# Planner thresholds per stage instead of per kernel, new rates and priorities, and a later padding memset in a two-layer attention-plus-mixer kernel

## The chip, the cores and the metric

The kernel runs on one core of one Trainium2 chip, whose engines run side by side, each with its own queue: PE (matrix multiply), ScalarE or ACT (activation functions), VectorE or DVE (elementwise work and reductions), GpSimd or POOL, and SyncE or SP, which here issues most of the transfers. The metric is the device time of one execution in microseconds (us).

## The reference

Two layers, each an attention block and a mixer block, over 2048 positions of width 448, with 16 heads of width 28 and a hidden width of 1792.

```python
def _A_ref(x, wqkv, wo):
    qkv = (x @ wqkv).reshape(B, S, 3, H, Dh).transpose(2, 0, 3, 1, 4)
    q, k, v = qkv[0], qkv[1], qkv[2]
    scores = jnp.einsum("bhqd,bhkd->bhqk", q, k) * (Dh ** -0.5)
    p = _softmax(scores, axis=-1)
    o = jnp.einsum("bhqk,bhkd->bhqd", p, v)
    return o.transpose(0, 2, 1, 3).reshape(B, S, D) @ wo

def _B_ref(x, w1, w2, w3, w4):
    h = _gelu(_layernorm(x, axis=-1) @ w1)
    hs = shifted(h) @ w2        # the four quarters of h moved by -1, +1, -2, +2 positions
    x1 = x + hs
    return x1 + _gelu(_layernorm(x1, axis=-1) @ w3) @ w4

for _ in range(2):
    x = x + _A_ref(_layernorm(x, axis=-1), A_wqkv, A_wo)
    x = x + _B_ref(_layernorm(x, axis=-1), B_w1, B_w2, B_w3, B_w4)
```

(`shifted` stands for the padding and slicing of the reference.)

## The kernel before

**Tiles.** Positions come in tiles of 128 rows. Queries are cut into five chunks a layer (4, 4, 4, 2 and 2 tiles), heads into four groups `g` of four. A *segment* is one chunk of queries, one head group and one range of key tiles; `ORDER` lists the ranges, 8 in layer 0 and 9 in layer 1, and each gives four segments (one per head group), so there are 68 segments. Four consecutive segments with the same chunk and range are called a *stage* here: 17 stages, numbered 0 to 16; a segment's number divided by four is its stage. In the trace a stage ends with every fourth copy of the output sums out of PSUM (lines 1838 and 1840).

**Blocks.** A *block* is a 128x512 tile of scores of one head: 2048 in all. `t_scores` (line 1629) walks the blocks in order in *units* that use alternate PSUM banks: an even unit has up to three banks (0, 1, 2), an odd one two (3, 4), or three when it is *widened* into bank 5. PE computes the scores (line 1487), ScalarE the exponentials of a whole unit in one instruction (`t_exp`, line 1754), PE the products with V (`t_pv`, line 1795, shown by the trace at the helper's line 831), VectorE copies the sums out.

**VectorE's share.** Some blocks are not sent to ScalarE. VectorE computes their exponentials by integer and polynomial steps: `d_first` (line 1582, one step at line 1584, reads PSUM) and `d_chain` (line 1595, seven steps, lines 1611 to 1624). A block gets there in two ways. *Ring*: in an even unit with two blocks, if VectorE's planned load over the last 3 us is under `XPAR['dt']` (line 1687), a later block is computed into bank 2 in place of the third. *Extra*: if PE's planned idle share over the last 8 us is at least `XPAR['ft']` (line 1723), a later block goes to a spare bank. In both, `ahead_of` (line 1640) looks 6 to 8 or 5 to 7 rows of four blocks ahead, into the next segment at most; it takes at most two of four blocks of a row, and in a segment no more than `rate * (row + 1) * 4`, with `rate` from `R_RATE` or `D_RATE`, which have one value per two segments. A staging buffer (two, and two more in some phases) and an output buffer (four, and one more) must be free. `XPAR['wt']` is the idle share from which an odd unit is widened (line 1681).

**The plan.** No instruction is placed by hand. Generators such as these ask a planner (`Sched`), while the program is built, for one instruction at a time; it keeps a time for each engine from written-down durations, picks by earliest start and by priority (a small number goes first), and so fixes each engine's order. Nothing of this runs on the chip: thresholds and priorities only change which instructions there are and their order. Priorities: `XPAR['rp']` for the first step of a ring block, `XPAR['dp']` for the seven steps of the chain (1.0 once they are due, `urge`, line 1603), `RANK` for the work of the layers (keys: `q`, `k`, `v` projections, `o` output projection, `a` and `b`, `c` the mixer, `w` the last matmul, `l` the layernorm; then layer and chunk). When PE would idle, the planner adds *fillers*, matmuls whose result nobody reads (line 2267); the idle share is counted in them.

**Other names the change touches.** `('mg', L, ch)` is the gelu mode of a chunk's first mixer half (`MODE`, line 586): 0 is a tanh formula, four steps on ScalarE with the exponential's table (line 2036) and two or three steps on VectorE or POOL each; 1 is one gelu together with the session of an earlier tile group; 2 is one gelu of its own. A gelu *session* needs a table load before and after (line 2018 or 2220, then 1754). For chunk 0, mode 1 means 0. `ek`, `eo`, `eq`, `ez`, `ex` say whether a small elementwise step goes to POOL (0), VectorE (1) or to whichever the planner finds sooner (2) (`both`, line 804). `l2` is the segment at whose start the weights `w3` and `w4` are fetched (lines 879 to 882). `Q_LEAD` is how many segments ahead a chunk's queries may be fetched (line 1379); `PE_NORM` picks how a chunk's sums are normalized. `t_setup_act` writes the padding columns of `vaug` (lines 954 to 965): the first four slots on ScalarE, the rest with two memsets on POOL.

Of the kernel before, what the change touches and what calls it, by code (L numbers as in the profile page):

```python
# [551 lines left out]
R_RATE = {(0,): 0.075, (1,): 0.197, (2,): 0.05, (3,): 0.031, (4,): 0.041, (5,): 0.042, (6,): 0.005, (7,): 0.105, (8,): 0.04, (9,): 0.089, (10,): 0.057, (11,): 0.143, (12,): 0.011, (13,): 0.09, (14,): 0.016, (15,): 0.219, (16,): 0.295, (17,): 0.149, (18,): 0.037, (19,): 0.217, (20,): 0.143, (21,): 0.087, (22,): 0.056, (23,): 0.13, (24,): 0.076, (25,): 0, (26,): 0, (27,): 0.127, (28,): 0.195, (29,): 0.058, (30,): 0.27, (31,): 0.199, (32,): 0.11, (33,): 0.103}  # L552
# [3 lines left out]
DWIN = 3.0  # L556
# [5 lines left out]
RANK = {('q', 0, 1): 1.184, ('q', 0, 2): 2.642, ('q', 0, 3): 2.141, ('q', 1, 0): 2.346, ('q', 1, 1): 2.061, ('q', 1, 2): 2.505, ('q', 1, 3): 2.755, ('b', 0, 0): 1.875, ('b', 0, 1): 1.316, ('b', 0, 2): 2.036, ('b', 0, 3): 2.897, ('b', 0, 4): 1.082, ('b', 1, 0): 2.902, ('b', 1, 1): 3, ('b', 1, 2): 2.351, ('b', 1, 3): 2.02, ('b', 1, 4): 1.926, ('a', 0, 0): 1.662, ('a', 0, 1): 1.144, ('a', 0, 2): 2.238, ('a', 0, 3): 1.371, ('a', 0, 4): 1.312, ('a', 1, 0): 1.017, ('a', 1, 1): 1.0, ('a', 1, 2): 1.499, ('a', 1, 3): 1.403, ('a', 1, 4): 2.715, ('k', 0, 1): 2.645, ('k', 0, 2): 2.042, ('k', 0, 3): 1.655, ('k', 1, 0): 2.274, ('k', 1, 1): 1.444, ('k', 1, 2): 1.666, ('k', 1, 3): 1.894, ('k', 1, 4): 2.34, ('c', 0, 0): 1.669, ('c', 0, 1): 1.339, ('c', 0, 2): 2.666, ('c', 0, 3): 2.96, ('c', 0, 4): 2.415, ('c', 1, 0): 2.208, ('c', 1, 1): 1.895, ('c', 1, 2): 1.744, ('c', 1, 3): 1.689, ('c', 1, 4): 1.841, ('w', 0, 0): 2.341, ('w', 0, 1): 1.863, ('w', 0, 2): 2.645, ('w', 0, 3): 2.29, ('w', 0, 4): 2.306, ('w', 1, 0): 2.293, ('w', 1, 1): 2.856, ('w', 1, 2): 2.827, ('w', 1, 3): 1.977, ('w', 1, 4): 2.705, ('o', 0, 0): 2.763, ('o', 0, 1): 2.676, ('o', 0, 2): 1.428, ('o', 0, 3): 2.55, ('o', 0, 4): 2.591, ('o', 1, 0): 1.304, ('o', 1, 1): 1, ('o', 1, 2): 2.597, ('o', 1, 3): 1, ('o', 1, 4): 2.482, ('v', 0, 1): 1.144, ('v', 0, 2): 1.659, ('v', 0, 3): 2.683, ('v', 1, 0): 1.215, ('v', 1, 1): 2.171, ('v', 1, 2): 1.452, ('v', 1, 3): 1.717, ('v', 1, 4): 2.499, ('l', 1, 0): 2.748, ('l', 1, 1): 1.813, ('l', 1, 2): 2.651, ('l', 1, 3): 2.514, ('l', 1, 4): 1.196}  # L562
Q_LEAD = {(0, 1): 60, (0, 2): 76, (0, 3): 71, (1, 0): 98, (1, 1): 54, (1, 2): 8, (1, 3): 13}
# [37 lines left out]
def build_kernel(nc, A_x, A_wqkv, A_wo, B_x, B_w1, B_w2, B_w3, B_w4, out, n_layers=2):  # L601
# [79 lines left out]
    with st:  # L681
# [272 lines left out]
        def t_setup_act():  # L954
# [5 lines left out]
            yield ("sig", ("vinit0",))  # L960
            yield ("wait", ("start",))
            rest = [("vaug", s) for s in range(4, NKV)]
            yield op("pool", 1.3, lambda e: e.memset(pads[:, 64:, 28:32], 0.0), writes=rest)
            yield op("pool", 0.5, lambda e: e.memset(pads[:, 64:, 28:29], 1.0), writes=rest)
            yield ("sig", ("vinit",))

# [615 lines left out]
        def d_first(blk, bank, ys, pd, ring=None):  # L1582
# [5 lines left out]
            else:  # L1588
                yield ("dead", bank)
                yield ("sig", ("dx", ring))  # L1590
            yield ("spawn", d_chain(blk, ys, pd), XPAR['dp'])

        at = [0, 0]

# [34 lines left out]
        def t_scores():  # L1629
# [40 lines left out]
            while True:  # L1670
# [62 lines left out]
                for blk, got in extra:  # L1733
                    yield ("spawn", d_first(blk, *got), 1 if len(got) == 3 else XPAR["rp"])
# [636 lines left out]
```

## Time and profile before

| what | value |
| --- | --- |
| median of 3 runs | 1029.54 us (1027.8 to 1031.02) |
| the profiled execution | 1027.66 us |
| its span, first to last instruction | 1025.8 us |
| ScalarE busy | 976.8 us |
| PE busy (fillers among it) | 974.6 us |
| VectorE busy | 812.9 us |
| POOL busy | 217.6 us |

A row of a group of instructions reads: line, engine, operation, output and inputs with their shapes, count, then busy time and the mean of one in ns, then the idle time of the engine just before them and what ended it. A row of a timeline reads: start, duration, engine, line, operation, shapes, count. A row of busy time by stretch gives the stretch, its length, and for the chosen engines the busy time with the number of instructions, then PE's granted clock as a share of full speed, the share of the transfer engines and GB/s.

### The profile page before, as it was taken

How to read it: one execution, taken by the hardware profiler on the slowest of the kernel's cores; microseconds unless marked ns; L12 is line 12 of the kernel's file. 1: busy time of each engine (PE TensorE's matmuls, PEld its weight loads, DVE VectorE, ACT ScalarE, POOL GpSimd, SP SyncE). 2: the span in 40 equal slices, each digit the busy share in tenths (PEclk: the TensorE clock that was granted, in tenths of full speed). 3: DMA queues.
4: the chain of work that ended last, by engine and by line, in shares of the span. 5: the costliest groups of instructions: out<-in, count | busy, mean ns of one | idle time of the engine just before them, and what ended most of it. 6: DMA issues, size and time to landing. Idle time of an engine off the chain costs nothing.

```text
span 1025.8 us, 36344 instructions
## 1 busy us (share of the span) xinstructions
PE 974.6 (95%) x16163; PEld 407.5 (40%) x16166; DVE 812.9 (79%) x2012; ACT 976.8 (95%) x897; POOL 217.6 (21%) x348
## 2 busy tenths in 40 slices
PE   8999999999999989999899999999899999899998
PEld 4323434333343344434334433334234333344465
DVE  8877997788768867896787867899798887887742
ACT  6899999999999999999999999999999999999952
POOL 3015020321114013241223100101333020221011
PEclk9999999999999999999999999999999999999999
DMA  4533552301013113321122124324302021121001
GB/s 126 130 73 116 114 166 73 74 25 43 12 28 89 42 36 79 52 54 24 28 71 65 43 71 136 116 75 111 82 16 49 13 52 35 33 56 45 13 12 33
DMA packets 98828, 64.42 MB, mean 63 GB/s; under 512 B 70832, under 2 KB 87552, under 8 KB 98672
## 3 DMA queue, kind: packets, MB, share of 16 engines
q1 hardware_dynamic: 94176, 53.11, 20.8%
q0 software_dynamic: 3376, 8.09, 3.0%
q8 instruction: 126, 2.06, 0.8%
q10 hardware_dynamic: 1120, 0.92, 0.3%
q14 instruction: 30, 0.25, 0.1%
HBM read 28.16 MB, written 16.76 MB: 44 GB/s over the span
## 4 chain that ended last, share of the span: by engine, by line
ACT 71%; PE 22%; DVE 6%; issue 1%; DMA 0%; POOL 0%; DVEq 0%; ACTq 0%
ACT PT L1754 64%; PE ps L840 12%; PE ps L1487 5%; PE ps L831 4%; ACT h2T L2220 3%; ACT fb L2036 1%; PE ps L2267 1%; ACT L1754 1%; ACT L2220 1%; ACT hT L2018 0%; DVE yd L1584 0%; DVE qT L1288 0%; DVE st L1050 0%; DVE vaug L1333 0%; ACT kT L2220 0%
## 5 line engine op out<-in xcount | busy, mean ns | idle before, releaser
L1754 ACT ACTIVATE PT<-ps 128x1024 bf16<-128x1024 f32 (+1 forms) x790 | 883.8, 1309 | 8.3 <-PE ps L1487 6.6
L1487 PE MATMUL ps<-qT,kT 32*128 32x512 bf16 (+1 forms) x2560 | 308.8, 340 | 25.3 <-ACT PT L1754 18.7
L831 PE MATMUL ps<-PT,vaug 128*32 128x512 bf16 (+1 forms) x2418 | 242.9, 342 | 0.6 <-DVE ub L1840 0.4
L1487 PEld LDWEIGHTS ps<-qT,kT 32*128 32x128 bf16 x2560 | 79.3, 91 | 295.6 <-ACT PT L1754 266.2
L840 PE MATMUL ps<-xT,w 128*32 128x512 bf16 (+4 forms) x2592 | 177.2, 344 | 4.1 <-DVE hT L2005 2.3
L2267 PE MATMUL ps<-ident 128*32 128x256 bf16 x2632 | 121.2, 279 | 1.9 <-POOL ident L930 1.5
L831 PEld LDWEIGHTS ps<-PT,vaug 128*32 128x32 bf16 x2418 | 72.5, 95 | 89.5 <-issue 73.0
L1865 POOL TENSOR_TENSOR otn<-ub,fb 128x512 bf16<-128x512 f32 (+1 forms) x31 | 34.4, 1110 | 283.4 <-DMA fb<-rscr 275.1
L840 PE MATMUL ps<-w,h2T 128*32 128x448 bf16 x1288 | 89.7, 355 | 4.2 <-ACT h2T L2220 4.0
L840 PEld LDWEIGHTS ps<-xT,w 128*32 128x32 bf16 (+1 forms) x2592 | 68.4, 95 | 56.2 <-issue 27.0
L2267 PEld LDWEIGHTS ps<-ident 128*32 128x32 bf16 x2632 | 75.7, 98 | 25.0 <-issue 9.7
L1584 DVE TENSOR_SCALAR yd<-ps 128x512 int16<-128x512 f32 x84 | 57.6, 686 | 24.6 <-PE ps L1487 24.0
L2196 DVE CAST h2T<-ps 128x384 bf16<-128x384 f32 (+1 forms) x84 | 52.2, 621 | 26.6 <-PE ps L840 25.5
L840 PEld LDWEIGHTS ps<-w,h2T 128*32 128x32 bf16 x1288 | 34.2, 96 | 32.9 <-issue 13.8
L840 PE MATMUL ps<-wo_pad,otn 128*32 128x448 bf16 x512 | 39.5, 356 | 2.2 <-DVE x1b L2105 0.8
L1615 DVE TENSOR_TENSOR fb<-fb 128x512 bf16<-128x512 int16 x96 | 40.3, 425 | 0.6
L840 PE MATMUL ps<-xT,wq_pad 128*32 128x512 bf16 x448 | 39.8, 382 | 0.9 <-DVE kT L1226 0.8
L840 PE MATMUL ps<-xT,wk_pad 128*32 128x512 bf16 (+1 forms) x512 | 39.5, 369 | 0.5 <-DVE vaug L1333 0.5
L840 PE MATMUL ps<-wv,xT 128*32 128x448 bf16 x480 | 36.9, 355 | 1.3 <-DVE vaug L1333 0.5
L2267 PE MATMUL ps<-ident,xn 128*32 128x256 bf16 x836 | 38.0, 276 | 0.0
L840 PE MATMUL ps<-w,hT 112*32 112x448 bf16 x512 | 36.6, 355 | 1.5 <-ACT hT L2018 1.3
L831 PE MATMUL ps<-PD,vaug 128*32 128x512 bf16 (+1 forms) x128 | 37.3, 344 | 0.0
(238 smaller groups left out, 1290.2 us busy)
## 6 DMA issues: line engine op xcount, KB each, us to landing
uscr<-ub SPq DMA_DIRECT2D x28, 256.0 KB
ub<-uscr SPq DMA_DIRECT2D x28, 256.0 KB
fb<-rscr SPq DMA_DIRECT2D x96, 64.0 KB, 2.0
xnd<-xn SPq DMA_DIRECT2D x28, 128.0 KB, 2.1
x_res<-in_A_x_dram POOLq DMA_DIRECT2D x16, 224.0 KB, 3.5
xd<-x_res SPq DMA_DIRECT2D x16, 224.0 KB, 3.3
x_res<-xd SPq DMA_DIRECT2D x16, 224.0 KB, 3.4
out_dram<-obf SPq DMA_DIRECT2D x16, 112.0 KB
```

The costliest lines, as they stand in the source:

```text
L831: return lambda e: e.matmul(out=out, lhsT=lhsT, rhs=rhs, start=start, stop=stop, **kw)
L840: r.append(e.matmul(out=out[c:c + w, :], lhsT=lhsT[:, c:c + w], rhs=rhs, start=start, stop=stop, tile_position=(0, c)))
L1487: yield op("pe", (0.005 + NW * 0.00042) / nc_, lambda e, i=i, kc=kc, j=j, g=g, a=a, NW=NW, bank=bank: e.matmul(out=ps[:, bank, i * NW:(i + ...
L1584: yield op("dve", c_ps(512), lambda e: e.tensor_scalar(out=y.bitcast(I16)[:, 0:512], in0=ps[:, bi(bank), :], scalar1=SCALE * L2E * FS, sca ...
L1615: yield op("dve", D_[2], lambda e: e.tensor_tensor(out=z, in0=qa, in1=qa, op=ALU.mult), reads=fk, writes=fk, urge=urge, two=True)
L1754: yield op("act", 0.0635 + n * w * 0.000833, lambda e, bk=bk, s0=s0, n=n, w=w: e.activation(out=PT[:, s0:s0 + n, 0:w], in_=ps[:, bk[0]:bk[ ...
L1865: yield both(("eo", L, ch), 0.2 + NW * 0.0021, 0.07 + NW * 0.00104, lambda e: e.tensor_tensor(out=otn[:, g, 0:NW], in0=u, in1=rb[:, 0:NW], ...
L2036: yield op("act", c_act(NW), lambda e: e.activation(out=f, in_=f, func=ACT.Tanh, scale=8.0 * GK * (2.0 / math.pi) ** 0.5), reads=[fk], wri ...
L2196: ev = op("dve", c_ps(m * NW), lambda e, hr=hr, pv=pv: e.tensor_copy(out=hr, in_=pv), reads=[("ps", bi(b))], writes=hk, touch=[b])
L2220: yield op("act", c_act(len(fr_) * NW), lambda e, v=v: e.activation(out=v, in_=v, func=ACT.Gelu_apprx_tanh), reads=allk, writes=allk, tab= ...
L2267: return [e.matmul(out=ps[32 * c:32 * c + 32, bi(b), 0:256].rearrange("p (a n) -> p a n", n=128), lhsT=xn[:, 0, D:D + 32] if live else ide ...
```

## The change

The code changes in seven places: six reads of `XPAR` get the stage as a second key, and the first of the two memsets in `t_setup_act` is declared to read the first query tile, so that it comes after it.

```diff
-            yield op("pool", 1.3, lambda e: e.memset(pads[:, 64:, 28:32], 0.0), writes=rest)
+            yield op("pool", 1.3, lambda e: e.memset(pads[:, 64:, 28:32], 0.0), reads=[("qT", 0, 0)], writes=rest)
...
-            yield ("spawn", d_chain(blk, ys, pd), XPAR['dp'])
+            yield ("spawn", d_chain(blk, ys, pd), XPAR["dp", blk[0] // 4])
...
-                return 1.0 if past else XPAR['dp']
+                return 1.0 if past else XPAR["dp", blk[0] // 4]
...
-                if u % 2 == 1 and SC.idle_share(8.0) >= XPAR['wt']:
+                if u % 2 == 1 and SC.idle_share(8.0) >= XPAR["wt", at[0] // 4]:
...
-                    if len(un) == 2 and u % 2 == 0 and rb is None and SC.load("dve", DWIN) < XPAR['dt']:
+                    if len(un) == 2 and u % 2 == 0 and rb is None and SC.load("dve", DWIN) < XPAR['dt', un[-1][0] // 4]:
...
-                if SC.idle_share(8.0) >= XPAR['ft']:
+                if SC.idle_share(8.0) >= XPAR["ft", si0 // 4]:
...
-                    yield ("spawn", d_first(blk, *got), 1 if len(got) == 3 else XPAR["rp"])
+                    yield ("spawn", d_first(blk, *got), 1 if len(got) == 3 else XPAR["rp", si0 // 4])
```

The rest is numbers. `R_RATE`, `D_RATE`, `RANK`, `Q_LEAD` and `PE_NORM` get new values almost throughout; `RANK` stays between 1 and 3. In `XPAR`, `l2` goes from 15 to 16, `('mg', 0, 0)` from 0 to 1, `('mg', 1, 0)` from 1 to 2, `('mg', 1, 4)` from 0 to 1, and about half of the `ek`, `eo`, `eq`, `ez` and `ex` values change. The five single values were `ft` 0.14, `dt` 0.658, `wt` 0.166, `rp` 0.322 and `dp` 3.06. The new ones stand at the right of this table of the stages; its middle columns are of the trace before: the stretch of the span, and how many blocks VectorE did in it (instructions of line 1584).

| stage | layer, chunk | key tiles | us | blocks | by VectorE | `ft` | `dt` | `wt` | `rp` | `dp` |
| --- | --- | --- | --- | --- | --- | --- | --- | --- | --- | --- |
| 0 | 0, 0 | 0-4 | 15-54 | 64 | 2 | 0.146 | 0.742 | 0.173 | 1.476 | 2.391 |
| 1 | 0, 1 | 0-4 | 54-83 | 64 | 1 | 0.146 | 0.628 | 0.173 | 1.131 | 2.567 |
| 2 | 0, 0 | 4-8 | 83-112 | 64 | 3 | 0.088 | 0.931 | 0.173 | 0.876 | 3.028 |
| 3 | 0, 0 | 8-16 | 112-164 | 128 | 14 | 0.157 | 0.713 | 0.198 | 0.794 | 2.175 |
| 4 | 0, 1 | 4-16 | 164-248 | 192 | 12 | 0.124 | 0.834 | 0.173 | 0.794 | 3.2 |
| 5 | 0, 2 | 0-16 | 248-366 | 256 | 17 | 0.146 | 0.726 | 0.329 | 0.794 | 1.584 |
| 6 | 0, 3 | 0-16 | 366-433 | 128 | 5 | 0.146 | 0.895 | 0.173 | 0.875 | 2.869 |
| 7 | 0, 4 | 0-16 | 433-490 | 128 | 6 | 0.041 | 0.621 | 0.163 | 1.296 | 2.931 |
| 8 | 1, 0 | 0-7 | 490-549 | 112 | 4 | 0.164 | 0.514 | 0.293 | 0.857 | 2.378 |
| 9 | 1, 1 | 0-7 | 549-611 | 112 | 3 | 0.146 | 0.772 | 0.171 | 0.794 | 3.2 |
| 10 | 1, 0 | 7-11 | 611-638 | 64 | 2 | 0.115 | 0.784 | 0.38 | 0.842 | 3.2 |
| 11 | 1, 1 | 7-11 | 638-666 | 64 | 5 | 0.039 | 0.935 | 0.059 | 0.794 | 3.081 |
| 12 | 1, 0 | 11-16 | 666-699 | 80 | 9 | 0.072 | 0.934 | 0.3 | 0.661 | 2.56 |
| 13 | 1, 1 | 11-16 | 699-735 | 80 | 4 | 0.183 | 0.521 | 0.23 | 0.661 | 3.055 |
| 14 | 1, 2 | 0-16 | 735-855 | 256 | 20 | 0.149 | 0.861 | 0.163 | 0.794 | 3.2 |
| 15 | 1, 3 | 0-16 | 855-919 | 128 | 6 | 0.146 | 0.55 | 0.173 | 0.794 | 3.2 |
| 16 | 1, 4 | 0-16 | 919-975 | 128 | 4 | 0.146 | 0.703 | 0.372 | 0.621 | 3.116 |

The queries' holds, with the first segment of each chunk's queries in the comment:

```diff
-Q_LEAD = {(0, 1): 60, (0, 2): 76, (0, 3): 71, (1, 0): 98, (1, 1): 54, (1, 2): 8, (1, 3): 13}
+Q_LEAD = {(0, 1): 7, (0, 2): 102, (0, 3): 50, (1, 0): 86, (1, 1): 54, (1, 2): 9, (1, 3): 71}
 # first segments: 4, 20, 24, 32, 36, 56, 60
```

More of the change, by code (lines that the diff above doesn't have):

```diff
@@ L566 @@
+PE_NORM = {(0, 0): False, (0, 1): False, (0, 2): False, (0, 3): False, (0, 4): False, (0, 5): True, (0, 6): False, (0, 7): True, (1, 0): False, (1, 1): False, (1, 2): False, (1, 3): False, (1, 4): False, (1, 5): True, (1, 6): False, (1, 7): False}
 Sched.AGED = 0
```

9 lines of the change are left out of this document (4 added, 5 removed).

## The prediction

> **What bounds the kernel now.** I read the page first (busy shares, then the chain that ended last), then the groups with shapes kept apart, then busy time by stretches.
>
> ```profile
> span 1025.8 us, 36344 instructions
> PE 974.6 (95%) x16163; PEld 407.5 (40%) x16166; DVE 812.9 (79%) x2012; ACT 976.8 (95%) x897; POOL 217.6 (21%) x348
> ...
> ACT 71%; PE 22%; DVE 6%; issue 1%; DMA 0%; POOL 0%; DVEq 0%; ACTq 0%
> ...
> L1754 ACT ACTIVATE PT<-ps 128x1024 bf16<-128x1024 f32 (+1 forms) x790 | 883.8, 1309 | 8.3 <-PE ps L1487 6.6
> ```
>
> `PE 974.6 (95%)` hides filler matmuls, so PE's share says little. ScalarE holds 71% of the chain; its exponentials alone (line 1754) take 883.8 us and wait 8.3 us in the whole run. The time is therefore ScalarE's work, plus a head before the first exponential and a tail after the last. What can the change move? The forms of the exponential tell.
>
> ```profile
> L1754 ACT ACTIVATE PT<-ps 128x1536 bf16<-128x1536 f32 x351 | 532.7, 1547 | 6.5 <-PE ps L1487 5.0 <-PE ps L831 1.1
> L1754 ACT ACTIVATE PT<-ps 128x1024 bf16<-128x1024 f32 x439 | 467.7, 1119 | 1.8 <-PE ps L1487 1.6
> ...
> L1584 DVE TENSOR_SCALAR yd<-ps 128x512 int16<-128x512 f32 x84 | 57.6, 686 | 24.6 <-PE ps L1487 24.0
> ...
> L1584 DVE TENSOR_SCALAR vaug<-ps 128x512 int16<-128x512 f32 x33 | 22.6, 685 | 12.0 <-PE ps L1487 12.0
> ```
>
> A block is 128x512 scores. ScalarE does 351 x 3 + 439 x 2 = 1931 of the 2048; VectorE does 84 + 33 = 117 with its own eight-step chain. A block taken from a three-bank exponential saves 1547 - 1119 = 428 ns; one taken from the stream saves the average, 883.8 / 1931 = 0.458 us. I use 0.44 us per block. What a block costs VectorE, from start to start:
>
> ```profile
> 691.05 0.68 DVE L1584 TENSOR_SCALAR yd<-ps 128x512 int16<-128x512 f32 x1
> 691.65 0.28 DVE L1611 TENSOR_SCALAR vaug<-vaug 128x512 uint16<-128x512 uint16 x1
> 691.85 0.28 DVE L1611 TENSOR_SCALAR fb<-vaug 128x512 uint16<-128x512 uint16 x1
> ...
> 697.68 0.41 DVE L1621 TENSOR_TENSOR vaug<-vaug 128x512 int16<-128x512 int16 x1
> 698.02 0.41 DVE L1619 TENSOR_TENSOR fb<-fb,vaug 128x512 bf16<-128x512 bf16 x1
> ```
>
> 0.60 for the first step, 0.20 for each of four tensor-scalar steps, 0.34 for each of three tensor-tensor steps: 2.42 us. Is there room? VectorE's busy time, stretch by stretch (a column of time and of share of DMA follows):
>
> ```profile
> 112.00:164.00 52.00, 46.53 (x125) 1.00 0.49 128
> 248.00:366.00 118.00, 90.69 (x222) 1.00 0.17 39
> 666.00:699.00 33.00, 32.41 (x86) 1.00 0.31 87
> 699.00:735.00 36.00, 31.90 (x84) 1.00 0.36 93
> ...
> sum 960.00, DVE 781.81; mean DVE 45.99
> ```
>
> 81% over the 960 us of exponentials: 77% in the large stage from 248, but 89%, 98% and 89% in the three stretches at 112, 666 and 699. There is room, and there are places with none.
>
> **The change, part by part.**
>
> *Edits that do nothing, and why.* `PE_NORM` changes only at chunk numbers 5 to 7; there are five chunks a layer. `mg` at (0,0) stays mode 0, and at (1,4) belongs to the last chunk, which goes direct. `Q_LEAD`: in five of seven places both values give the same first segment (clamped at 0, or unchanged); for (1,2) the hold moves from segment 48 to 47, for (1,3) from 47 to 0, but these loads first wait for the output sums of segments 48 and 52. Counted at nothing, by the code.
>
> *Padding set later.* The two memsets move behind the first `qT`. Now they run here:
>
> ```profile
> 10.20 0.16 DVE L1009 TENSOR_TENSOR sc<-sc,wsum 128x4 f32<-128x4 f32 x1
> ...
> 11.49 1.05 DVE L1011 TENSOR_SCALAR sc<-sc 128x4 f32<-128x4 f32 x1
> ...
> 12.72 0.68 DVE L1238 TENSOR_REDUCE kmaxc<-ps 128x1 f32<-128x512 f32 x1
> ...
> 11.41 1.11 POOL L963 MEMSET vaug<- 128x1216 bf16 x1
> 12.57 1.45 POOL L964 MEMSET vaug<- 128x304 bf16 x1
> 20.95 0.24 POOL L1056 TENSOR_SCALAR rstd<-mv 128x4 f32<-128x4 f32 x1 [6.93 <-DVE mv L1051]
> ```
>
> A 128x4 step that takes 0.16 us takes 1.05 beside the first memset. That holds the reduction of line 1238, on which the first query bias waits, until 12.72; its input, a matmul of the same stretch, was there little sooner. I take -0.1 us, between 0 and -0.9 (1.05 - 0.16, were all of it on the path). Behind the waiting memsets POOL's next work starts only at 20.95, after 6.93 us idle; 2.6 us of memset fit, so the move costs nothing. Without that cover `rstd` would be late by up to 2.6 us.
>
> *The MLP weights one segment later* (`l2` 15 to 16): three transfers on POOL's queue.
>
> ```profile
> L880 POOL DMA_DIRECT2D w<-in_B_w_dram x1: 791/791/791, 141.4 to 141.4; - x1
> ...
> 242.26 1.03 PE L840 MATMUL ps<-xT,w 128*32 128x384 bf16 x16
> ```
>
> First use is 101 us after the issue; a segment here is about 52 / 4 = 13 us. Zero; if the cover were gone, 13 us at one place.
>
> *Gelu of layer 1's first chunk* (`mg` (1,0) from 1, which for chunk 0 means 0, to 2): four tanh steps on ScalarE become one gelu session with its own two table loads. An existing session and an existing tanh step:
>
> ```profile
> 823.92 1.28 ACT L2018 ACT_TABLE_LOAD   x1
> 825.22 1.91 ACT L2018 ACTIVATE hT<-hT 112x2048 bf16<-112x2048 bf16 x1
> ...
> 831.72 1.28 ACT L1754 ACT_TABLE_LOAD   x1
> ...
> 901.15 0.65 ACT L2036 ACTIVATE fb<-fb 112x512 f32<-112x512 f32 x1
> 901.67 2.38 ACT L1754 ACTIVATE PT<-ps 128x1024 bf16<-128x1024 f32 x2
> ```
>
> Session 1.28 + 1.91 + 1.28 = 4.47; tanh 4 x (901.67 - 901.15) = 2.08. ScalarE pays +2.4 us. If it falls next to another session the loads are shared and it pays 1.91 - 2.08 = -0.2. VectorE loses two steps per group (lines 2035, 2037), which I count as room and not as time. The Trainium skill ("ScalarE: Activation LUTs", What ACT_TABLE_LOAD costs) puts a switch at about 2.66 us, the load and a drain of 1.38; by it the session would be 2.8 us dearer and the sum 1024. The row does not bear this out: the load starts at 823.92, where the exponentials before it end, and the next activation follows within 0.02 us of the load's end.
>
> *The thresholds and rates.* This is the main term. A block goes to VectorE when PE's planned idle share is at least `ft`, or when VectorE's planned load is under `dt`, subject to rates and buffers. `dt` rises from 0.658 in 12 of 17 stages (mean of the new values 0.745) and falls in 5; `ft` falls from 0.14 in 6 (mean 0.127). The rates' mean goes from 0.102 to 0.119 (`R_RATE`) and from 0.260 to 0.228 (`D_RATE`). Worked out from the diff segment by segment (at most rate x blocks, rounded up, and two of four blocks in a row), the rates allowed 746 blocks and now allow 670, against 117 done. So the gates decide, and on the whole they open. By how much no row shows. Bounds: from below, 20 blocks fewer (+8.8 us), if the lower `D_RATE` and the five tighter stages rule; from above, VectorE at 90% of the 960 us: 864 - 781.8 = 82 us, 82 / 2.42 = 34 more (-15 us). Between these I take +20: the wider gate `dt` governs 790 / 2 = 395 even units, of which at least 44 (395 - 351) lose a bank to VectorE now; that is the larger lever, it is loosened in three quarters of the stages, and VectorE ends at (781.8 + 48) / 960 = 86%, under what the three full stretches already bear. 20 x 0.44 = -8.8 us.
>
> *Priorities* (`RANK`, `dp`, `rp`, engine choice of small steps): they reorder work beside the exponentials. Its cover is ScalarE's own queue; where it fails ScalarE waits, as in two stretches now (columns: PE, PEld, VectorE, ScalarE, POOL):
>
> ```profile
> 420.00:465.00 45.00, 41.94 (x757) 17.42 (x759) 39.21 (x88) 43.64 (x41) 16.63 (x25) 1.00 0.20 45
> 680.00:750.00 70.00, 64.04 (x915) 23.54 (x912) 60.77 (x151) 68.00 (x60) 16.21 (x20) 0.98 0.31 80
> ```
>
> 1.4 and 2.0 us are lost. Zero taken; -3.4 if both close, +10 if three more such stretches open to three times that. `rp` rises from 0.322 to 0.62 or more, yet stays under the 1 of most layer work except in three stages.
>
> *The tail.* The last exponential ends at 974.5; then PE bounds:
>
> ```profile
> 983.14 6.36 PE ps L840 x144
> ...
> 1004.92 18.02 PE ps L840 x408
> ```
>
> No instruction there is changed; whether a tile group falls before or into the tail may be. A 128-row tile has 56 matmuls of the kind in these rows, 18.02 / 408 = 44 ns each, 2.5 us; a group of four is 10 us. Zero taken, between -10 and +10.
>
> **Sum**, on the profiled execution's 1027.66 us (its span of 1025.8 and 1.9 around it; the median 1029.54 is 1.9 above it): 1027.66 - 0.1 + 2.4 - 8.8 = 1021.2. I forecast 1021 us.
>
> **The rivals.**
>
> *A. More of the same, and a shorter tail*: 34 blocks (-15) and half a group out of the tail (-5) with the session at +2.4: 1010. For it: VectorE's 77% in the large stages. Against: nothing aims at the tail.
>
> *B. The gates are not what limits*: the look-ahead window of three blocks, two staging buffers and four output buffers refuse, and the count stays at 117. Then only the session and the padding count: 1027.66 + 2.3 = 1030, no change to speak of. For it: the old rates already allowed far more than 117. Against: the count by stage is uneven, which fixed buffers alone would not give.
>
> *C. VectorE becomes the bound where PE idles most; slower.* `ft` opens when PE idles, and PE's fillers (line 2267) are thickest just where VectorE is full:
>
> ```profile
> 112.00:164.00 52.00, 24.06 (x504) 14.54 (x494) 1.00 0.49 128
> 666.00:699.00 33.00, 12.96 (x252) 7.53 (x248) 1.00 0.31 87
> 699.00:735.00 36.00, 8.09 (x172) 5.17 (x172) 1.00 0.36 93
> ```
>
> Slack of VectorE in these three: 5.5 + 0.6 + 4.1 = 10.2 us, 4 blocks. If 12 more land here, 29 - 10 = 19 us go on the path; other stages give back 8 x 0.44 = 3.5, the session costs 2.4, and half the 19 is made good later, since work not done here delays no exponential in stages with room: 1027.66 + 9.5 - 3.5 + 2.4 = 1036. It decides from the fifth added block in these stretches. For it: `ft` in the stage at 666 goes from 0.14 to 0.072 and `dt` to 0.934. Against: in the stage at 699 `dt` falls to 0.521 and the `D_RATE` cap is cut, and at 112 `ft` rises to 0.157.
>
> **Chances.** Forecast 0.45 (its own range 1015 to 1026), A 0.15, B 0.15, C 0.25. About 0.3% (3 us) is what a measurement of this kernel can tell from no change. The forecast and A are faster: 0.60. B is split 0.10 same and 0.05 slower, C is slower: 0.30. Range 1010 to 1037: it takes in A's point and C's, and leaves out the far half of each.
>
> **What would show it.** Right: L1584 counts 137 or so instead of 117, three-bank exponentials fall, VectorE near 86%, one more pair of table loads with three 112x2048 gelus on line 2018 (two now) and four fewer tanh steps, line 1011 at about 0.16 us, the exponentials still waiting under 10 us. Wrong: L1584 at 117 or fewer (B); or the chain of waits running through VectorE and ScalarE idle by more than 10 us between 112 and 164 or 666 and 735 (C); or a tail that is not 51 us long.

## The result, and the profile after

| | before | after |
| --- | --- | --- |
| median of 19 runs each, us | 1027.45 | 1025.36 |
| lowest to highest, us | 1025.71 to 1031.02 | 1024.38 to 1026.27 |
| the profiled execution, us | 1027.66 | 1025.66 |
| its span, us | 1025.8 | 1023.9 |

The ratio is 0.9979, with a 95% interval from 0.9971 to 0.9986: faster by 0.2%, where the forecast of 1021 was 0.6% under the 1027.66 that it started from. First the page of the changed kernel (busy times, shares of the chain, the exponentials), then its groups with shapes kept apart (columns as before: busy us, mean ns, idle before and its releaser).

```profile
span 1023.9 us, 36349 instructions
PE 973.4 (95%) x16102; PEld 404.7 (40%) x16102; DVE 843.5 (82%) x2134; ACT 973.6 (95%) x897; POOL 220.1 (21%) x350
...
ACT 62%; PE 23%; DVE 12%; DMA 1%; issue 1%; ACTq 0%; SPq 0%; DVEq 0%
...
L1754 ACT ACTIVATE PT<-ps 128x1024 bf16<-128x1024 f32 (+1 forms) x791 | 877.8, 1288 | 7.8 <-PE ps L1487 6.6
```

```profile
L1754 ACT ACTIVATE PT<-ps 128x1536 bf16<-128x1536 f32 x332 | 503.2, 1540 | 5.9 <-PE ps L1487 5.3
L1754 ACT ACTIVATE PT<-ps 128x1024 bf16<-128x1024 f32 x459 | 482.3, 1106 | 1.8 <-PE ps L1487 1.3
...
L1584 DVE TENSOR_SCALAR yd<-ps 128x512 int16<-128x512 f32 x94 | 64.5, 686 | 21.8 <-PE ps L1487 21.1
L1584 DVE TENSOR_SCALAR vaug<-ps 128x512 int16<-128x512 f32 x40 | 27.3, 685 | 4.6 <-PE ps L1487 4.4
L2036 ACT ACTIVATE fb<-fb 112x512 f32<-112x512 f32 x12 | 8.4, 731 | 0.0
L2018 ACT ACTIVATE hT<-hT 112x2048 bf16<-112x2048 bf16 x3 | 5.7, 1914 | 0.0
```

Line 1584 counts 94 + 40 = 134 blocks on VectorE, 17 more and not 20; the three-bank exponentials fall from 351 to 332, and all exponentials together from 883.8 to 877.8 us of ScalarE, 6.0 and not 8.8. The session is there (three gelus of 112x2048, twelve tanh steps of 112x512 where there were sixteen).

To see where the rest went, the span is cut at the first and the last exponential, and ScalarE's time between them is cut again: from the start of each instruction to the start of the next, counted for exponentials (what they wait is in it) and for everything else on ScalarE. All later tables use these four parts; for the two kernels, in us:

| part | before | after | change |
| --- | --- | --- | --- |
| up to the first exponential | 15.27 | 15.16 | -0.1 |
| exponentials, with their waits | 883.6 | 877.4 | -6.2 |
| ScalarE's other work between them | 75.6 | 77.9 | +2.3 |
| tail, from the end of the last exponential | 51.4 | 53.5 | +2.1 |
| span | 1025.85 | 1023.92 | -1.9 |

The head and the session cost what the prediction said. The exponentials give 6.2 where 8.8 were counted, and a tail that was counted at zero takes 2.1. The exponentials' change holds more than the blocks: the time that ScalarE sits idle in the middle of the run is in it too, and that differs between executions of one order by 0.6 us in one case below (the late gate) and 1.9 in another (the session alone). The head first, VectorE's step that had run beside POOL's memset:

```profile
11.66 0.17 DVE L1011 TENSOR_SCALAR sc<-sc 128x4 f32<-128x4 f32 x1
```

The step takes 0.17 us where it took 1.05, but the work behind it had waited for little of this: the first exponential starts 0.1 us sooner. Now ScalarE's busy time, stretch by stretch, first a row of the kernel before, then three of the changed one; behind them all engines of the changed one (PE, PEld, VectorE, ScalarE, POOL) where rival C saw no room:

```profile
120.00:220.00 100.00, 99.99 (x90) 1.00 0.32 87
```

```profile
120.00:220.00 100.00, 98.13 (x86) 1.00 0.37 94
...
420.00:465.00 45.00, 44.71 (x43) 1.00 0.37 52
...
680.00:750.00 70.00, 69.62 (x65) 1.00 0.33 81
```

```profile
112.00:164.00 52.00, 47.72 (x799) 20.39 (x795) 49.88 (x131) 51.97 (x46) 13.22 (x16) 1.00 0.38 112
666.00:699.00 33.00, 30.64 (x480) 12.48 (x477) 32.16 (x86) 32.62 (x30) 5.96 (x5) 1.00 0.35 98
699.00:735.00 36.00, 34.97 (x514) 12.95 (x510) 28.09 (x64) 36.00 (x34) 11.26 (x17) 1.00 0.38 83
```

The two leaks that the prediction left open have closed (44.71 of 45 instead of 43.64, 69.62 of 70 instead of 68.00) and one has opened (98.13 of 100 instead of 99.99). VectorE is not the bound in the three narrow stretches: ScalarE is busy for 51.97, 32.62 and 36.00 us of them. What, then, is the tail's 2.1? PE's matmuls of line 840 in the tail (the kernel before, then after), and after's fillers, the matmuls that the planner adds where PE would idle (line 2267; none in the tail before):

```profile
974.47:1025.80 51.33, 45.63 (x1068) 1.00 0.07 23
```

```profile
970.46:1023.90 53.44, 45.54 (x1096) 1.00 0.09 25
...
970.46:1023.90 53.44, 1.68 (x36) 1.00 0.09 25
```

The work is the same (45.63 and 45.54 us); 1.7 of the 2.1 us is PE without work, painted over by fillers. The transfers that transpose the layernorm's output for line 840 suggest why: the last pair of them starts 1.9 us before the last exponential ends (968.57 to 970.46), where before it was 9.5 us ahead (965.02 to 974.47).

```profile
965.02 3.53 SPq L1075 DMA_TRANSPOSE xT<-xn  x2
```

```profile
968.57 3.13 SPq L1075 DMA_TRANSPOSE xT<-xn  x2
```

So where the last sums are normalized, in small steps on VectorE and PE (lines 1838 and 1881), PE had this tile group's matmuls to do in between before, and has fillers now. The same steps of PE's timeline, before and after:

```profile
976.60 0.27 PE L1881 MATMUL ps<-identf,rs 128*8 128x128 f32 x1
976.60 0.28 PE L840 MATMUL ps<-xT,w 128*32 128x256 bf16 x3
976.71 0.27 PE L1881 MATMUL ps<-identf,rs 128*8 128x128 f32 x1
976.71 0.82 PE L840 MATMUL ps<-xT,w 128*32 128x256 bf16 x17
```

```profile
972.34 0.28 PE L1881 MATMUL ps<-identf,rs 128*8 128x128 f32 x1
972.42 0.29 PE L2267 MATMUL ps<-ident 128*32 128x256 bf16 x3
972.46 0.27 PE L1881 MATMUL ps<-identf,rs 128*8 128x128 f32 x1
972.54 0.62 PE L2267 MATMUL ps<-ident 128*32 128x256 bf16 x13
```

### The profile page after: what moved, and what is told of

The parts are those of the page before. It is cut to its first block, busy times and chain, and to the rows that moved or that the text cites. A ratio compares the mean times of both kernels' runs of the same rounds, so it can differ in the third digit from the quotient of the medians.

```text
span 1023.9 us, 36349 instructions
## 1 busy us (share of the span) xinstructions
PE 973.4 (95%) x16102; PEld 404.7 (40%) x16102; DVE 843.5 (82%) x2134; ACT 973.6 (95%) x897; POOL 220.1 (21%) x350
## 4 chain that ended last, share of the span: by engine, by line
ACT 62%; PE 23%; DVE 12%; DMA 1%; issue 1%; ACTq 0%; SPq 0%; DVEq 0%
ACT PT L1754 55%; PE ps L840 12%; PE ps L1487 5%; PE ps L831 4%; ACT h2T L2220 3%; PE ps L2267 1%; ACT fb L2036 1%; DVE yd L1584 1%; DMA xT<-xnd 1%; DVE fb L1619 1%; DVE fb L1615 1%; DVE PD L1624 1%; DVE ub L1840 1%; DVE vaug L1621 1%; ACT L1754 1%
## 5 line engine op out<-in xcount | busy, mean ns | idle before, releaser
L1754 ACT ACTIVATE PT<-ps 128x1024 bf16<-128x1024 f32 (+1 forms) x791 | 877.8, 1288 | 7.8 <-PE ps L1487 6.6
L840 PE MATMUL ps<-xT,w 128*32 128x512 bf16 (+3 forms) x2592 | 178.7, 343 | 1.7 <-issue 0.8
L2267 PEld LDWEIGHTS ps<-ident 128*32 128x32 bf16 x2508 | 73.1, 98 | 25.3 <-issue 9.2
L1584 DVE TENSOR_SCALAR yd<-ps 128x512 int16<-128x512 f32 x94 | 64.5, 686 | 21.8 <-PE ps L1487 21.1
L1865 POOL TENSOR_TENSOR otn<-ub,fb 128x512 bf16<-128x512 f32 (+1 forms) x32 | 37.2, 1162 | 189.3 <-DMA fb<-rscr 178.7
L2196 DVE CAST h2T<-ps 128x384 bf16<-128x384 f32 (+1 forms) x84 | 52.0, 619 | 19.7 <-PE ps L840 17.9
L1615 DVE TENSOR_TENSOR fb<-fb 128x512 bf16<-128x512 int16 x112 | 49.0, 438 | 0.7
L831 PE MATMUL ps<-PD,vaug 128*32 128x512 bf16 (+1 forms) x146 | 43.9, 342 | 1.2 <-DVE PD L1624 1.0
L2267 PE MATMUL ps<-ident,xn 128*32 128x256 bf16 x896 | 40.8, 274 | 0.6 <-DVE ub L1840 0.6
L1621 DVE TENSOR_TENSOR yd<-yd,fb 128x512 int16<-128x512 int16 x88 | 38.3, 436 | 1.2
L840 PE MATMUL ps<-xT,wq_pad 128*32 128x512 bf16 x448 | 36.8, 382 | 1.4 <-DVE kT L1226 0.8
```

The lines of the kernel that those rows point to most:

```text
L831: return lambda e: e.matmul(out=out, lhsT=lhsT, rhs=rhs, start=start, stop=stop, **kw)
L840: r.append(e.matmul(out=out[c:c + w, :], lhsT=lhsT[:, c:c + w], rhs=rhs, start=start, stop=stop, tile_position=(0, c)))
L1584: yield op("dve", c_ps(512), lambda e: e.tensor_scalar(out=y.bitcast(I16)[:, 0:512], in0=ps[:, bi(bank), :], scalar1=SCALE * L2E * FS, sca ...
L1615: yield op("dve", D_[2], lambda e: e.tensor_tensor(out=z, in0=qa, in1=qa, op=ALU.mult), reads=fk, writes=fk, urge=urge, two=True)
L1621: yield op("dve", D_[5], lambda e: e.tensor_tensor(out=ya, in0=ya, in1=z, op=ALU.add), reads=yk + fk, writes=yk, urge=urge, two=True)
L1754: yield op("act", 0.0635 + n * w * 0.000833, lambda e, bk=bk, s0=s0, n=n, w=w: e.activation(out=PT[:, s0:s0 + n, 0:w], in_=ps[:, bk[0]:bk[ ...
```

## The experiments

Two theories. *Theory 1* is the prediction's way of counting: the parts of the change have prices, the prices add up along ScalarE, and head, waits and tail are constants. *Theory 2*: each edit makes the planner deal out the whole order anew from the point where it first acts, so that waits and tail move by amounts of their own, larger than the prices. Times are medians; the difference in the last column is against runs of the kernel before on the same chip; the parts are those of the profiled execution, cut as above (before: 15.3, 883.6, 75.6, 51.4).

| run | blocks | head | exponentials | other | tail | time | against before |
| --- | --- | --- | --- | --- | --- | --- | --- |
| no vector blocks | 0 | 15.2 | 928.6 | 75.4 | 56.3 | 1078.25 | +50.7 |
| gelu session alone | 121 | 16.8 | 882.5 | 78.0 | 58.1 | 1037.01 | +8.4 |
| padding alone | 117 | 17.6 | 883.5 | 75.6 | 51.4 | 1027.38 | -0.2 |
| gates alone | 124 | 16.6 | 883.9 | 80.5 | 53.7 | 1036.97 | +9.4 |
| after, old gates | 120 | 16.5 | 894.4 | 79.6 | 54.8 | 1045.63 | +17.0 |
| after, tanh | 133 | 14.8 | 878.1 | 74.3 | 71.0 | 1039.68 | +12.1 |
| weights later alone | 113 | 15.3 | 895.9 | 77.1 | 56.6 | 1046.77 | +18.1 |
| the same, queries first | 112 | 15.7 | 886.7 | 76.3 | 58.3 | 1039.22 | +12.2 |
| one rank by 0.01 | 133 | 15.1 | 897.6 | 81.7 | 59.8 | 1056.62 | +28.0 |
| one tail priority | 134 | 15.2 | 876.1 | 77.9 | 64.0 | 1035.18 | +7.4 |
| one late gate | 127 | 15.7 | 880.7 | 77.9 | 58.5 | 1033.43 | +5.6 |
| seven late numbers | 133 | 15.6 | 878.2 | 77.9 | 52.0 | 1024.45 | -3.3 |

### What a block, the session and the padding cost

**No blocks on VectorE** (the kernel before, all rates at zero):

```diff
-R_RATE = {(0,): 0.075, (1,): 0.197, ...}
-D_RATE = {(0,): 0, (1,): 0.169, ...}
+R_RATE = {(0,): 0, (1,): 0, ...}
+D_RATE = {(0,): 0, (1,): 0, ...}
```

> Before, with all values of R_RATE and D_RATE set to 0, so that ScalarE computes all 2048 blocks and VectorE none (117 fewer there). Theory 1 (the time is ScalarE's sum plus a fixed head and tail; parts add up): the last exponential ends 117 x 0.43 = 50 us later than before's 974.5, at 1025, the tail stays at 51 us, the time is about 1078 us. Theory 2 (every edit deals the whole order anew, so waits and tail change by amounts of their own): the exponentials end near 1025 too, but the tail is off 51 us by 5 us or more in either direction.

1078.25 us, ratio 1.0489 (1.0473 to 1.0506). Its groups:

```profile
L1754 ACT ACTIVATE PT<-ps 128x1536 bf16<-128x1536 f32 x450 | 681.9, 1591 | 3.9 <-PE ps L1487 3.4
L1754 ACT ACTIVATE PT<-ps 128x1024 bf16<-128x1024 f32 x349 | 399.6, 1145 | 0.3 <-PE ps L1487 0.2
```

450 x 3 + 349 x 2 = 2048 banks. The exponentials with their waits grow by 928.6 - 883.6 = 45.0 us for 117 blocks, 0.385 us each; but ScalarE's idle time before them falls from 8.3 to 3.9 + 0.3 = 4.2 us, and without it they grow by 49.1, 0.42 us a block. The price of a block is a little under the 0.44 of the prediction. The tail grows by 5, which no block explains. The time is Theory 1's 1078, but by luck: the last exponential ends at 1019 and not at 1025, and the longer tail makes up for it.

**The gelu session alone** (the kernel before, its numbers put under the per-stage keys unchanged):

```diff
-('mg', 1, 0): 1
+('mg', 1, 0): 2
```

> Before, with only the gelu mode of layer 1's first chunk changed from tanh steps to a session of its own; 121 blocks by VectorE (117 in before). Theory 1: 2.4 us more for the session, 1.7 us less for four blocks, so the same time as before within 2 us. Theory 2: slower by 5 us or more; ScalarE's work without exponentials grows by about 2.3 us and the rest of the loss is waits and tail.

ScalarE's other work grows by 2.4 us, the price of the prediction to the tenth. (By the Trainium skill, "ScalarE: Activation LUTs", What ACT_TABLE_LOAD costs, two switches of 2.66 us would make it about 5.2, an estimate; the drain that the Trainium skill adds to a load is not seen here either, where the load, the gelu and the load back take 4.5 us from 756.16 to 760.68.) The exponentials are 1.1 shorter, but not by the 4 blocks more: at 755 us, where ScalarE's order is still that of before, they are 1.9 shorter already, which is a difference between two executions of one order. Yet the time is 8.4 us longer. In the profiled execution 1.5 is a later head, again in the order of before, and 6.7 is the tail: up to the end of stage 13 its stages take as long as before, then the planner deals differently. In its tail, line 840 and the fillers:

```profile
977.29:1035.30 58.01, 47.80 (x1134) 1.00 0.10 23
...
977.29:1035.30 58.01, 3.17 (x96) 1.00 0.10 23
```

2.2 us more of line 840 have fallen into the tail, 3.2 are fillers, and 1.0 more is idle.

**The padding alone:**

```diff
-            yield op("pool", 1.3, lambda e: e.memset(pads[:, 64:, 28:32], 0.0), writes=rest)
+            yield op("pool", 1.3, lambda e: e.memset(pads[:, 64:, 28:32], 0.0), reads=[("qT", 0, 0)], writes=rest)
```

> Before, with only the padding memsets moved behind the first query tile. The order on every other engine is the same. Theory 1 and 2 alike: line 1011 takes about 0.17 us instead of 1.05, the first exponential starts 0.1 us sooner, the time does not change measurably (ratio within 0.1% of 1). If instead a later place hurts, POOL's memsets stretch other VectorE steps between 14 and 18 us and the first units start later.

1027.38 us, ratio 1.0001 (0.9991 to 1.0011). Line 1011 takes 0.17 us, as expected, and from the first exponential on the profile is the kernel before's to within 0.15 us. The first exponential itself starts 2.4 us later in this execution and not 0.1 sooner; the last section takes that up. So the 0.1 us is not shown by this run, only that the padding does not move the time by more than the interval.

### The halves of the change

**The gates alone**: the kernel before with the new `R_RATE`, `D_RATE`, `ft`, `dt` and `wt`, the rest unchanged.

> Before, with only the new rates and the per-stage thresholds ft, dt and wt (priorities, modes and engine choices as before); VectorE gets 124 blocks instead of 117. Theory 1: 7 x 0.43 = 3 us faster than before, about 1024 us. Theory 2: slower than before, 1032 us or more, with the loss in the tail or in ScalarE's waits and not in its sum.

**The rest without the gates**: the changed kernel with the old ones.

> After, with the old rates and the old ft, dt and wt in all stages (new priorities, modes and engine choices kept); 120 blocks by VectorE. Theory 1: 14 x 0.43 = 6 us slower than after, 1031 us. Theory 2: slower by more than that, 1038 us or more, with the excess over 6 us in waits, ScalarE's other work and tail.

The gates alone: 1036.97, ratio 1.0091 (1.0071 to 1.0111), with 7 blocks more than before. The rest alone: 1045.63, ratio 1.0175 (1.0157 to 1.0193). Both halves lose, by 9.4 and 17.0 us, and together they win 2.1. No sum of prices for the parts does that. The gates alone also move only 7 blocks of the 17, and with them the exponentials, with their waits, do not get shorter (883.9 and 883.6); the loss is 4.9 in ScalarE's other work, 2.3 in the tail and 1.3 in the head. In the rest alone the longest of ScalarE's waits is

```profile
556.03 4.62 ACT L1754 ACTIVATE PT<-ps 128x1536 bf16<-128x1536 f32 x4 [7.04 <-PE ps L1487]
```

**The changed kernel with the tanh steps** instead of the session:

```diff
-('mg', 1, 0): 2
+('mg', 1, 0): 1
```

> After, with the gelu mode of layer 1's first chunk put back to tanh steps (133 blocks by VectorE, 134 in after). Theory 1: the session's 2.4 us of ScalarE come back and nothing else moves, 1023 us (2 us faster than after). Theory 2: ScalarE's part ends 2 to 3 us sooner but the tail is dealt anew; a tail longer than after's 53 us by more than 5 us, and the time above 1030 us, would show it.

1039.68, ratio 1.0116 (1.01 to 1.0132). The last exponential ends at 967.16, 3.3 us sooner than in the changed kernel, and the tail is 17.5 us longer. Theory 2's signs came, and it is work that has fallen into the tail: 18.3 us more of line 840 than the changed kernel's 45.54, and no fillers.

```profile
967.16:1038.10 70.94, 63.86 (x1460) 1.00 0.12 31
```

Four tanh steps of a late tile group stand there too, and ScalarE waits for VectorE before them (5.24 us before the first, at 972.40); whether they held the group back was not tested.

### Edits that were counted at nothing

**The weights one segment later, alone** (the kernel before):

```diff
-'l2': 15
+'l2': 16
```

> Before, with only l2 from 15 to 16 (the fetch of w3 and w4 one segment later); VectorE gets 113 blocks (117 in before). The prediction priced this at nothing, since the first use is 101 us after the issue. Theory 1: 4 x 0.43 = 2 us slower at most, 1029 us. Theory 2: slower by 10 us or more although no instruction waits for these weights, because POOL's order after the fetch, and with it everything else, is dealt anew.

1046.77, ratio 1.0178 (1.0158 to 1.0197). The issue on line 880 is now at 151.9 us, it lands in 8.1, and the trace shows no instruction that waited for it: the cover that the prediction named holds. But the order is another one: a step of line 1865 that ran on POOL behind the fetch (159.7 us) now runs ahead of it (150.7), VectorE's order differs from about 155 us on, and 6.60 us are lost at one place:

```profile
554.31 5.97 ACT L1754 ACTIVATE PT<-ps 128x1536 bf16<-128x1536 f32 x5 [6.60 <-PE ps L1487]
```

The score matmuls there lack their queries. These are written by line 1288; its instructions between 480 and 570 us in the kernel before, here, and in the next run (count, then shortest, median and longest ns, first and last start):

```profile
L1288 DVE TENSOR_SCALAR qT<-ps,bc x4: 739/742/751, 525.9 to 536.2; 128x512 bf16<-128x512 f32 x4
```

```profile
L1288 DVE TENSOR_SCALAR qT<-ps,bc x4: 744/748/751, 549.6 to 556.2; 128x512 bf16<-128x512 f32 x4
```

```profile
L1288 DVE TENSOR_SCALAR qT<-ps,bc x4: 742/750/751, 536.7 to 543.7; 128x512 bf16<-128x512 f32 x4
```

**The same with the queries first**, to test that reading:

```diff
-'l2': 15
+'l2': 16
-('q', 1, 0): 2.346
+('q', 1, 0): 1.0
```

> The kernel before with l2 at 16 (as in the run with the weights later alone, 1046.8 us) and RANK of ('q', 1, 0), the query projection of layer 1's first chunk, from 2.346 to 1.0. In the run with the weights later alone ScalarE waits 6.6 us at 547.7 and 2.2 at 671.1 for score matmuls, and the queries of line 1288 are written there from 549.6 to 556.2 us, 20 us later than in the kernel before (525.9 to 536.2). If late queries are what the later weights cost in the stretch of exponentials: the queries are written before 545 us, both waits are gone, and the last exponential ends at about 978 us instead of 988.3. Theory 1 then adds the tail of before, 51.4 us: time about 1031 us. Theory 2: the mixer work that the queries overtook has to be done later, so the tail is longer than the 56.6 us of that run, by 3 us or more; time 1035 to 1042 us, still slower than before's 1027.5.

The queries come 13 us sooner, and both waits are gone. Where 6.60 us were lost, ScalarE now runs without a wait:

```profile
539.39 21.55 ACT L1754 ACTIVATE PT<-ps 128x1536 bf16<-128x1536 f32 x19
```

It does so at 671 us too. The last exponential ends at 978.70 (expected: about 978), and the time is 1039.22, ratio 1.012 (1.0103 to 1.0137), inside Theory 2's 1035 to 1042 and 8 us over Theory 1's 1031. The tail is 58.3, longer than the 56.6 of the run before by 1.7 and not by the 3 that were expected. That late queries made the wait is shown; the loss in the tail remains.

**One rank by 0.01** (the changed kernel):

```diff
-('q', 0, 1): 2.187
+('q', 0, 1): 2.197
```

> After, with one priority of 59 changed by 0.01: RANK of the query projection of layer 0, chunk 1, from 2.187 to 2.197. The built program gives VectorE 133 blocks (134 in after). Theory 1 (parts add up): one block, 0.4 us, so the same time as after within 1 us. Theory 2 (the order is dealt anew from the first instruction that changes places): the time moves by 10 us or more, slower, and the loss shows in ScalarE's waits, in extra work on ScalarE or in the tail, not in the number of blocks.

1056.62, ratio 1.0281 (1.0262 to 1.0301): the slowest but one of all runs, and about 31 us over the changed kernel, by a change of one priority in its third digit. 2.197 is above 2.195, the rank of `('k', 0, 1)`, and 2.187 is below it, so the query projection of chunk 1 now stands behind the key projection. ScalarE's busy time in the changed kernel and here:

```profile
16.00:60.00 44.00, 37.84 (x38) 1.00 0.34 86
60.00:120.00 60.00, 59.49 (x57) 1.00 0.42 111
```

```profile
16.00:60.00 44.00, 30.67 (x31) 1.00 0.39 97
60.00:120.00 60.00, 48.81 (x48) 0.94 0.32 72
```

17.9 us are lost in these two stretches (7.17 and 10.68), and the longest wait in them is

```profile
61.86 0.21 ACT L1432 ACTIVATE fct<-dbc 128x4 f32<-128x4 f32 x1 [9.09 <-DVE dbc L1461]
```

The queries of line 1288 are late here too: written from 56.0 to 74.2 us, in the changed kernel from 43.4 to 58.5. That they make all of the loss is not shown.

### The tail by itself

**One priority that acts only in the tail** (the changed kernel, the value of before):

```diff
-('b', 1, 3): 2.996
+('b', 1, 3): 2.02
```

> The changed kernel with one priority put back to the value of before: RANK of ('b', 1, 3), the mixer of layer 1's chunk 3, from 2.996 to 2.02. The planner's order of every engine is the changed kernel's until 4 us before the last exponential; behind that point the same instructions stand in another order, except for fillers. Theory 1 (the tail is a fixed amount of work with PE as its bound, so its length is a constant of the sum): last exponential ends at about 970.5 us, tail 53 to 54 us, time 1025 +-1 us. Theory 2 (the order decides how much of the tail's dependent steps are covered by other tile groups' matmuls): last exponential ends within 1 us of 970.5, and the tail alone grows, by about the matmul time of one tile group of four, 10 us, since one group then runs with nothing beside it: time about 1035 us.

1035.18, ratio 1.0068 (1.0055 to 1.0082), where Theory 2 said about 1035. PE's order is the changed kernel's until the output projection's matmuls 3 us behind the last exponential. That one ends at 969.16, and the tail is 64.0 us instead of 53.5. In it, line 840, then fillers, then a piece of the chain of waits (start, us, what):

```profile
969.16:1033.10 63.94, 45.14 (x1096) 1.00 0.08 21
...
969.16:1033.10 63.94, 10.05 (x296) 1.00 0.08 21
```

```profile
1007.91 0.56 DVE x1b L2105
...
1011.92 1.01 DVE xT L1096 x3
1012.92 0.04 issue
1012.97 17.26 PE ps L840 x392
```

PE has the same work as in the changed kernel (45.14 and 45.54 us), but does most of it before the last tile group's layernorm is begun. Then the chain runs through VectorE, step by step, and PE fills 10 us. The tail is not an amount of work; it is that work and a chain of dependent steps, and it is short when matmuls are kept back to lie beside the chain.

**One gate that first acts at 720 us** (the changed kernel):

```diff
-('dt', 14): 0.861
+('dt', 14): 0.658
```

> The changed kernel with one threshold put back to the value of before: dt of stage 14 from 0.861 to 0.658. Nothing differs before stage 14 (about 720 us). Blocks on VectorE by the build: 127 instead of 134. Theory 1: 7 blocks go back to ScalarE, 7 x 0.43 = 3.0 us more, nothing else: time 1028.4 us (range 1027 to 1030), tail 53.5. Theory 2: the 3.0 us are there, and the tail and the waits move too, because the work of the layers is dealt out anew from 720 us on: the tail leaves 53.5 us by more than 2 us, and the time is 1028.4 plus that.

1033.43, ratio 1.0049 (1.0034 to 1.0064). Seven blocks go back, the exponentials take 3.3 us more, and the tail 5.0 more, as Theory 2 had it; 0.5 is a later head. Of the 3.3, 0.6 stand ahead of the changed gate, where the order is the changed kernel's; the other 2.7 are 0.39 a block. Here it is work that has fallen into the tail, 53.25 us of line 840 and not 45.54 (7.7 us, three of the prediction's 2.5 us tiles), and there are no fillers:

```profile
974.28:1032.70 58.42, 53.25 (x1232) 1.00 0.09 25
```

**Seven late numbers**, found by varying only numbers that act late:

```diff
-R_RATE (30,): 0.071    RANK ('a', 1, 3): 2.129    RANK ('c', 1, 4): 2.718
+R_RATE (30,): 0.652    RANK ('a', 1, 3): 1.376    RANK ('c', 1, 4): 2.195
-('ex', 1, 11): 1    ('dt', 15): 0.55    ('wt', 15): 0.173    ('wt', 16): 0.372
+('ex', 1, 11): 0    ('dt', 15): 0.599    ('wt', 15): 0.195    ('wt', 16): 0.065
```

> The changed kernel with seven late numbers changed (R_RATE of segments 60 and 61, RANK of ('a', 1, 3) and ('c', 1, 4), the engine of one small step of tile 11, dt of stage 15, wt of stages 15 and 16), found by trying late numbers alone. 133 blocks on VectorE instead of 134. Theory 1: one block more on ScalarE, +0.4 us: time 1025.8 us, tail 53.5 us. Theory 2, with the tail as the term that gave back part of the gain: fewer fillers in the tail (36 matmuls, 1.7 us, in the changed kernel) and a tail 1 to 2 us shorter, near the 51.4 us of before; time 1024 us (range 1023 to 1025.5), 0.1 to 0.2% under the changed kernel.

1024.45, ratio 0.9968 (0.9955 to 0.998). The transposing transfers start at 963.66, 8.0 us before the last exponential ends, and no filler runs in the tail, which is 1.4 us shorter than the changed kernel's, with one block fewer on VectorE; both are as Theory 2 said. It is 0.9 us under the changed kernel; since the intervals of the two ratios overlap, it is not shown to be the faster of the two. The row of line 840 in its tail:

```profile
971.66:1023.70 52.04, 46.13 (x1088) 1.00 0.07 23
```

## Why the prediction was right or wrong

**What bounds the kernel: right.** ScalarE still carries most of the chain (62%, down from 71%; VectorE's share goes from 6% to 12%). Of the signs that the prediction named for being right, the blocks (134), VectorE's load (812.06 of 955.5 us, 85%), the session, line 1011 and the exponentials' waits under 10 us all came; so did one that it named for being wrong, a tail that is not 51 us long.

**Padding, session: right.** The session cost 2.3 in the change and 2.4 alone. The head of the changed kernel is 0.1 us shorter, which is less than the heads of two executions differ. The edits that do nothing were taken from the code; no run tests them apart.

**The thresholds: the direction right, the largest term mis-sized, the first step that failed.** 17 blocks instead of 20, and 6.2 us instead of 8.8, a miss of 2.6. The count: the prediction gave all its blocks to rates and gates, but the gates alone move 7, and taking them out of the changed kernel takes 14. So the 17 come from the gates and the new order together; which of the rates and thresholds moved them was not separated, except that one `dt` moves 7. The price: 0.36 us a block in the change (6.2 / 17), against 0.42 in the run without blocks and 0.39 in the one with the late gate. One execution cannot settle it: in the run with one tail priority PE's order is the changed kernel's until after the last exponential, and there the exponentials took 876.1 and not 877.4, which makes 0.44. The forms lie between. From start to start, where ScalarE waited for nothing, a three-bank exponential takes 1.33 us and a two-bank one 0.92 in both kernels, so 19 of the one fewer and 20 of the other more make 6.9 us, 0.41 a block. So the count was off by 3 blocks, 1.3 us, and the other 1.3 is as large as two executions of one order differ.

**Priorities counted at zero, between -3.4 and +10.** In the change the two stretches that I named did close, and a new leak of 1.9 us opened at 120 to 220 us. But "its cover is ScalarE's own queue" was wrong as a reason: one rank by 0.01 took that cover away and cost 31 us against the changed kernel, and a range of +10 was too narrow for what such an edit can do. That the term came out near zero was luck.

**The weights later, counted at zero.** The cover was right, nothing waited for them, and the price of the edit alone was still +18.1 us, through another order of the rest; 6.6 of it is the wait for late queries, and most of the remainder was not taken apart.

**The tail, counted at zero: the second step that failed, and the one whose reason was wrong.** The prediction asked only whether a tile group falls before or into the tail. In the change none did (45.63 and 45.54 us of line 840). What moved was how much of the tail's chain of small steps had matmuls beside it: 1.7 us of fillers. The run with one tail priority shows the same at five times the size (8.4 us more of fillers) without any change of work, and the seven late numbers, with no filler in the tail, take 1.4 us back. With the 2.6 us of the blocks, these 2.1 make up what was missed, less the 0.1 by which the session was cheaper: a fall of 6.5 was forecast and 1.9 came.

**The rivals.** A (a shorter tail) and C (VectorE bound at 112 and from 666 to 735) did not come; B (the gates are not the limit, the count stays) is refuted by the 134 blocks and by the one `dt` that moves 7. The rival that was missing is the one the halves showed: the change as a new order of everything. Nine runs gave the planner another order by one or two edits or by a half of the change (all but the padding, the seven late numbers and the run without blocks), and every one was slower than both kernels. The order of the changed kernel is not the sum of its edits, and its 2.1 us can be told from the trace only as a whole, by its four parts.

Not settled: why the planner's orders after the single edits come out longer as often as they did; that was not taken apart beyond the late queries, the late tile groups and the tail's chain. One reading that no run tests: if the numbers of both kernels were themselves picked by their time, as the seven late numbers were, almost any other order would be longer.

## What to carry to other kernels

Where a planner or a list scheduler places every instruction, price an edit as a new order and not as its own instructions: a single priority that crosses its neighbour was worth 31 us here, more than ten times what the whole change brought. Treat the tail as a chain of dependent steps with work to lay beside it, and look for fillers or idle PE in it before counting it as constant. The price of moving a unit of work off the bounding engine can be foretold (0.39 to 0.42 us against 0.44); how many units move, and what the rest of the order does meanwhile, has to be run.

## What the runs showed of the hardware

The kernel before does not always run at the full granted clock. Of its 36 executions beside these experiments, 20 had a mean of 0.997 or 0.998 (median 1028.0 us) and 16 had 1.0 (median 1026.7); all 19 of the changed kernel had 1.0. The profile shows where, in the execution of the kernel before (PE's busy time by stretches of 2 us, then the clock) and in that of the padding alone:

```profile
733.00:735.00 2.00, 1.22 (x13) 1.00 0.51 112
...
737.00:739.00 2.00, 2.00 (x31) 0.50 0.75 133
```

```profile
8.00:10.00 2.00, 0.42 (x9) 1.00 1.10 326
...
12.00:14.00 2.00, 2.00 (x24) 0.50 0.05 16
```

In both cases the clock is at half about 4 us after a stretch in which PE is busy for only 61% or 21% of 2 us. That is not yet a rule: in the same execution of the kernel before, PE is busy for 1.87 of the 3.40 us from 371.2, less than the 2.14 of the 3.40 us from 733.0, and the clock stayed at 1.00. In the first case this is the leak at 680 to 750 us that the change closed: PE waits there for exponentials again and again (six waits from 728 to 737 us, 2.5 us in all). In the second it is the head, and the first exponential starts at 17.64 instead of 15.27; but 1.0 of these 2.4 us is lost before the clock falls at 10.8 (the step of line 1004 starts at 9.87, before it was 8.86). Four profiled executions have such a dip in the head (gates alone; after, old gates; session alone; padding alone), and their first exponentials start at 16.5 to 17.6 us; in the other ten they start at 14.8 to 15.7.

The Trainium skill ("TensorE: Matmul & The Clock Gate", Part 1, What's actually happening) has the clock at half after an idle window of about 3.4 us, and full again after a busy one of the same length. The length of the dip agrees (0.15, 0.50 and 0.21 of three stretches of 2 us are lost, 1.7 us, or 3.4 us at half), but PE was not idle for so long: it was busy for 2.75 of the 4 us up to 737.

So of the 2.1 us between the medians, 1.3 remain when executions at the full clock are compared (1026.7 and 1025.4, from separate sets of runs); that the rest is the dip alone is argued from these medians and not shown by an experiment. The dip is also in the exponentials' 6.2 us: in the run with the session alone the clock stayed at 1.00 from 733 to 741 us, and its exponentials were 1.9 us shorter up to 755 us in the order of the kernel before. How much of the 6.2 is the dip was not separated.
